# Loads of q, k and v issued from POOL instead of SP, a second staging buffer for k, and q of the first tile in one piece

## The chip, the cores and the metric

The kernel runs on one core of one Trainium2 chip. The metric is device time in microseconds (us) of one execution; before the change it is 709.55 us, the median of three runs (708.3 to 709.76).

## What is computed

Attention with a bias, followed by two layers of the mixture kind (two matrices in, one out), over B = 2 batches, H = 8 heads, S = 576 positions, D = 64:

```python
scores = scale * np.matmul(q, k.transpose(0, 1, 3, 2))            # scale = 1/sqrt(D)
x = (log1p(abs(i - j)) / log1p(max(i, 1)))[..., None]
bias = np.maximum(x @ w1 + b1, 0.0) @ w2                          # 32 hidden, one column per head
attn = softmax(scores + bias.transpose(2, 0, 1)[None])
x = (attn @ v) as [1152 tokens, 512]
x = (x @ w_a) * (x @ w_b) @ w_out                                 # 512 -> 1536 -> 512
return silu(x @ w_gate) * (x @ w_val) @ w_out2
```

## The kernel before

All arithmetic is in 32-bit floats. Matmuls that need it are split into a high part that TensorE takes quickly and a low part (names that end in `a` and `b`, or in `h` and `l`), so a product is three matmuls.

**Bias units.** The bias depends on a row and a column position alone. It is made in 36 units of 16 rows for all 8 heads (`Bias.make`, line 132): four hidden layers `hd` (L122 on VectorE or L124 on ScalarE), matmuls against w2 on TensorE (L146), scaled copies into a tile `bt` (L128, L130), and a write of that tile to a scratch tensor `bias_d` in DRAM (L159, 295.5 KB, on SP's queue). Four units (32 to 35) are made ahead of everything; they are the bias rows of the tile t = 4.

**Attention.** The heads go in four pairs p = 0 to 3. The 1152 query columns (both batches) are cut into five tiles, in the order t = 4, 0, 1, 2, 3: t = 4 has 64 queries of each batch (192 columns of `qd` with 64 columns of zeros), the others 128 of each. A step is one (t, p), tile by tile, p inside; there are 20 steps. A step with t = 4 does both batches at once, in one half; the others have two halves. Before each half `make()` makes up to three bias units (three for each of the first four halves, then two and one in turn) until all 36 are there. The rows of a tile's bias can only be loaded once the units of that tile have been written.

In a step, for each of the two heads j, a tile `bt` (four buffers in all, L264's input) is loaded from `bias_d` on SP's queue: for t = 4 in two loads of 64 rows each (L355, 144 KB each, four loads in a step), else in one load of 128 rows (L352, 288 KB, two loads in a step). Then `scores` makes the matmuls of q and k (L259) in PSUM, VectorE adds the bias and takes the minimum (L264; the "score reduction" below), ScalarE makes the exponentials (L270), TensorE transposes them (L288), copies go to `ee` (L275, L277), TensorE multiplies with v (L299), and `finish` divides by the sums.

**Loads of heads.** `Heads` loads what a pair needs, all on SP's queue. `load_k(p)` (L187, 576 KB) fetches k into one staging buffer `kr` and splits it at once: a cast to `ka` (L172 on VectorE or L174 on ScalarE) and a subtraction to `kb` (L176, VectorE). `load_q(p, t)` (L182) does the same for q of one step (96 KB for t = 4, else 128 KB). `load_v(p)` (L192, 640 KB) fetches v, which isn't split; each pair has its own v tile.

At the start SP issues the constants `cs`, the logarithms `LW`, k0 and q of step 0, then v0. In step idx, after the step's bias row loads, SP issues k of the next pair (first tile only), q of the next step, and v of the next pair (first tile only). The lines of the loop:

```python
with tc.issue_after(load.ins):
    if idx + 1 < len(steps):
        if t == ORDER[0] and p < H // 2 - 1:
            heads.load_k(p + 1)
        heads.load_q(*steps[idx + 1])
        if t == ORDER[0] and p < H // 2 - 1:
            heads.load_v(p + 1)
```

`tc.issue_after(ins)` keeps what the block issues on the engine of `ins` behind `ins`, on that engine alone. The order of instructions on each engine is otherwise set by the framework's planner when the program is built, from its own estimates; each engine then takes its instructions strictly in that order and waits on semaphores. `Share` decides, from a running sum of estimated costs, whether a cast or copy goes to VectorE or ScalarE.

**The two layers** (`moe`, L404 the matmuls, L424 to L429 and L453 to L458 around them) follow; POOL computes there (L458) and at the very start.

Of the kernel before, what the change touches and what calls it, by code (L numbers as in the profile page):

```python
# [9 lines left out]
F32 = mybir.dt.float32  # L10
# [7 lines left out]
P = 128  # L18
B, H, S, D = 2, 8, 576, 64
# [9 lines left out]
ORDER = (4, 0, 1, 2, 3)  # L29
# [43 lines left out]
class Share:  # L73


    def __init__(self):
        self.spent = [0.0, 0.0]
# [14 lines left out]
class Bias:  # L92
# [7 lines left out]
    def __init__(self, tc, stack, cst, lm, bias_d, heads, share):  # L100
        nc = self.nc = tc.nc
        self.tc, self.bias_d, self.share = tc, bias_d, share
        bc = self.bc = stack.enter_context(tc.tile_pool(name="bm", bufs=1, side="right"))
        cs = bc.tile([P, 214], F32, name="cs")
        LW = self.LW = bc.tile([P, S], F32, name="LW")
        nc.sync.dma_start(cs, cst)
        last_load = nc.sync.dma_start(LW, lm)
        one = bc.tile([P, 1], F32, name="one")
        nc.gpsimd.memset(one, 0.0)
        nc.scalar.activation(one, one, AF.Exp)  # L110
        W1, B1, self.W2, PS, self.RE = cs[:, 0:1], cs[:, 1:2], cs[:, 2:34], cs[:, 34:178], cs[:, 178:214]
        with tc.high_priority():
            bp = self.bp = bc.tile([P, 144], F32, name="bp")
            nc.vector.tensor_scalar(bp, PS, B1, None, op0=ALU.mult)
            ready = nc.vector.tensor_scalar(LW, LW, W1, None, op0=ALU.mult)
        with tc.issue_after(ready.ins), tc.issue_after(last_load.ins):
            heads.load_k(0)
            heads.load_q(0, ORDER[0])

    def hidden(self, dst, n, m):  # L120
        if self.share.on_dve(n, DFAST):
            self.last = self.nc.vector.tensor_scalar(dst, self.LW[:, :n], self.bp[:, m : m + 1], 0.0, op0=ALU.add, op1=ALU.max)  # L122
        else:
            self.nc.scalar.activation(dst, self.LW[:, :n], AF.Relu, bias=self.bp[:, m : m + 1])  # L124
# [37 lines left out]
class Heads:  # L162


    def __init__(self, tc, pool, qd, kd, vd, share):
        self.nc, self.pool, self.d, self.got, self.share = tc.nc, pool, (qd, kd, vd), {}, share

    def split(self, raw, tags, bufs):
        w = raw.free_size() if hasattr(raw, "free_size") else raw.shape[1]
        hi, lo = (self.pool.tile([P, w], F32R, tag=x, name=x[:2], bufs=bufs) for x in tags)  # L170
        if self.share.on_dve(w, DFAST):
            self.nc.vector.tensor_copy(hi, raw)  # L172
        else:
            self.nc.scalar.copy(hi, raw)  # L174
        self.share.dve(w)
        self.nc.vector.tensor_tensor(lo, raw, hi.bitcast(F32), op=ALU.subtract)  # L176
        return hi, lo

    def load_q(self, p, t):
        s, n = (0, 192) if t == 4 else (192 + 256 * t, 256)  # L180
        raw = self.pool.tile([P, n], F32, tag=f"rawq{n}", name="rawq", bufs=1 if t == 4 else 2)
        self.nc.sync.dma_start(raw, self.d[0][p][:, s : s + n])  # L182
        self.got["q", p, t] = self.split(raw, (f"qa{n}", f"qb{n}"), 2)

    def load_k(self, p):
        kr = self.pool.tile([P, B * S], F32, tag="kr", name="kr", bufs=1)
        self.nc.sync.dma_start(kr, self.d[1][p])  # L187
        self.got["k", p] = self.split(kr, (f"ka{p}", f"kb{p}"), 1)

    def load_v(self, p):  # L190
        vv = self.pool.tile([P, B, 10, D], F32, tag=f"vv{p}", name="vv", bufs=1)
        self.nc.sync.dma_start(vv, self.d[2][p])  # L192
        self.got["v", p] = vv


# [35 lines left out]
def attention(ctx, tc, a4, heads, share, bias, units, bias_d, xh, xl, weights, ident):  # L231

    nc = tc.nc
    with (
# [6 lines left out]
        def bias_rows(h, t, n):  # L241
            e = bias_d[t][h]
            return bass.AP(tensor=e.tensor, offset=e.offset + 15, ap=[[16 * BW, n // 16], [BW - 1, 16], [1, S]])
# [3 lines left out]
        def scores(p, q, blocks, bt, sums):  # L247

            ka, kb = heads.got["k", p]
            qa, qb = q  # L250
            ps = ps2.tile([P, 2, 2, 512], F32, tag="big", name="ps")
            es = a4.tile([P, 2, S], F32, tag="es", name="es", bufs=3)
            for hf in range(2):
                for m, (lt, rt) in enumerate(((qa, ka), (qa, kb), (qb, ka))):
                    for j in range(2):
                        r = slice(64 * j, 64 * j + 64)
                        for n, (c0, b) in enumerate(blocks):
                            k0 = S * b + 288 * hf
                            nc.tensor.matmul(  # L259
                                ps[:, j, hf, :288], lt[r, c0 : c0 + P], rt[r, k0 : k0 + 288], start=m + n == 0, stop=m + n == len(blocks) + 1  # L260
                            )
            for j in range(2):
                nm = a4.tile([P, 1], F32, tag="nm", name="nm", bufs=4)
                nc.vector.tensor_tensor_reduce(  # L264
                    out=es[:, j].rearrange("p (a j) -> p a j", a=2), in0=ps[:, j, :, :288], in1=bt[j].rearrange("p (a j) -> p a j", a=2),
                    op0=ALU.add, op1=ALU.min, scale=-0.125, scalar=3.0e38, accum_out=nm,
                )
                share.dve(S, 1.3)
                share.act(S, 190.0)
                nc.scalar.activation(es[:, j], es[:, j], AF.Exp, bias=nm, scale=-1.0, accum_out=sums[:, j : j + 1])  # L270
            return es.rearrange("p h k -> p (h k)")
# [20 lines left out]
        def values(p, pu, ee, blocks):  # L292

            vv = heads.got["v", p]
            for cols, b, o in blocks:
                n = cols.stop - cols.start
                for kc in range(5):
                    for j in range(2):
                        nc.tensor.matmul(pu[64 * j : 64 * j + 64, o : o + n], vv[:, b, 5 * j + kc], ee[:, 4 * j + kc, cols], start=kc == 0, stop=kc == 4)  # L299
# [30 lines left out]

        for u in UNITS[:FIRST]:
            units.make(u, bank)
        heads.load_v(0)
        rest = list(UNITS[FIRST:])
        steps = [(p, t) for t in ORDER for p in range(H // 2)]
        half = 0

        def make():
            nonlocal half
            for _ in range(MADE[half] if half < len(MADE) else 0):  # L340
                if rest:
                    units.make(rest.pop(0), bank)
                    if not rest:
                        bias.close()
                        weights.pool = ctx.enter_context(tc.tile_pool(name="wpa2", bufs=1, side="right"))
            half += 1

        for idx, (p, t) in enumerate(steps):
            bt = [a4.tile([P, S], F32, tag="bias", name="bt", bufs=4) for j in range(2)]
            for j in range(2):  # L350
                if t < 4:
                    load = nc.sync.dma_start(bt[j], bias_rows(2 * p + j, t, P))  # L352
                else:
                    for b in range(B):
                        load = nc.sync.dma_start(bt[j][64 * b : 64 * b + 64], bias_rows(2 * p + j, 4, 64))  # L355
            with tc.issue_after(load.ins):
                if idx + 1 < len(steps):
                    if t == ORDER[0] and p < H // 2 - 1:
                        heads.load_k(p + 1)
                    heads.load_q(*steps[idx + 1])  # L360
                    if t == ORDER[0] and p < H // 2 - 1:
                        heads.load_v(p + 1)
                if idx == len(steps) - 2:
                    weights.load(3)
            q = heads.got["q", p, t]
            pu = ps0.tile([P, 512], F32, tag="pu", name="pu")
            if t < 4:
                sums = a2.tile([P, 2 * B], F32, tag="sums", name="sums")
                for b in range(B):
                    make()  # L370
                    es = scores(p, q, [(P * b, b)], bt, sums[:, 2 * b : 2 * b + 2])
                    values(p, pu, transposed(es), [(slice(0, P), b, P * b)])
            else:
                sums = a2.tile([P, 2], F32, tag="sums4", name="sums")
                make()
                es = scores(p, q, [(64 * b, b) for b in range(B)], bt, sums)
                values(p, pu, transposed(es), [(slice(64 * b, 64 * b + 64), b, 64 * b) for b in range(B)])
            finish(p, t, pu, sums)
# [159 lines left out]
```

## Time and profile before

| | |
|---|---|
| median of three runs | 709.55 us (708.3 to 709.76) |
| profiled execution, its own time | 708.51 us |
| its span, first to last instruction | 706.7 us |
| TensorE (PE) busy | 663.4 us, 94% of the span |
| VectorE (DVE), ScalarE (ACT), POOL busy | 65%, 46%, 2% |
| DMA | 71.44 MB, mean 101 GB/s; all of the program's on one queue |
| attention | to about 245 us; then the two layers |

An engine's busy time counts its instructions, not its waits. "Idle before" an instruction is how long its engine did nothing just ahead of it, and the arrow names what ended that. A granted clock of 1.00 is TensorE at 2.4 GHz, 0.50 at 1.2 GHz. The DMA share is the mean over the core's 16 DMA engines, so a quarter can be four engines that never rest.

### The profile page before, as it was taken

Reading aid. Unit: us, or ns where it says so; the run is one execution under the profiler, and the core shown is the slowest. Engines: PE = TensorE matmul, PEld = TensorE weight load, DVE = VectorE, ACT = ScalarE, POOL = GpSimd, SP = SyncE. Lnnn points to the kernel's source line nnn. Section 1 sums busy time; section 2 is a strip of 40 time slices with the busy share of each in tenths; the row PEclk is TensorE's granted clock in tenths of the full one; section 3 lists DMA queues with packets and bytes.
Section 4 is the critical chain, followed back from the end, with each engine's and each line's share of the span. In section 5 each row is a group of like instructions: output and inputs, shape, how many; then the busy total and the mean of one; then the engine's idle time right before and its main releaser. Section 6 shows DMA issues by size and latency. Waiting matters only on the chain.

```text
span 706.7 us, 11756 instructions
## 1 busy us (share of the span) xinstructions
PE 663.4 (94%) x4584; PEld 584.3 (83%) x4584; DVE 460.4 (65%) x1034; ACT 322.4 (46%) x675; POOL 13.9 (2%) x19
## 2 busy tenths in 40 slices
PE   6457799999999989999999999999999999999997
PEld 3133455655776879999999999999999999999997
DVE  5445688886777969999938961289923992342222
ACT  5514667775676747555415432265513641221110
POOL 0000000000000000000000001202000000000000
PEclk9767999999999999999999999999999999999999
DMA  4663554544335315444413430033510540000111
GB/s 134 186 199 123 155 145 132 155 125 115 100 101 156 102 60 179 148 151 128 142 59 94 146 119 1 1 107 124 163 55 1 157 141 0 1 1 1 45 45 45
DMA packets 27096, 71.44 MB, mean 101 GB/s; under 512 B 2720, under 2 KB 6944, under 8 KB 27040
## 3 DMA queue, kind: packets, MB, share of 16 engines
q1 hardware_dynamic: 27040, 70.68, 32.6%
q8 instruction: 36, 0.59, 0.3%
q14 instruction: 20, 0.16, 0.1%
HBM read 57.42 MB, written 13.25 MB: 100 GB/s over the span
## 4 chain that ended last, share of the span: by engine, by line
PE 83%; DMA 8%; DVE 4%; ACT 2%; issue 2%; SPq 1%; DVEq 0%; ACTq 0%
PE p L404 42%; PE po L404 21%; PE pu L299 6%; PE tp L146 5%; PE tp L288 5%; PE ps L259 4%; DMA rawq<-in_qd 3%; DMA kr<-in_kd 3%; DMA raw<-in_wm 1%; DMA bias_d<-bt 1%; PE tp L311 1%; DVE es L264 1%; DVE hd L122 1%; ACT es L270 1%; DMA LW<-in_lm 0%
## 5 line engine op out<-in xcount | busy, mean ns | idle before, releaser
L425 DVE TENSOR_TENSOR g<-p,g 128x384 f32<-128x384 f32 x72 | 40.0, 556 | 140.2 <-PE p L404 140.1
L404 PE MATMUL p<-xh,wh 128*128 128x384 f32 x288 | 96.7, 336 | 2.2 <-ACT g L424 2.2
L404 PE MATMUL p<-xl,wh 128*128 128x384 f32 x288 | 96.5, 335 | 0.0
L404 PE MATMUL po<-gh,wl 128*128 128x384 f32 x288 | 96.5, 335 | 0.0
L404 PE MATMUL p<-xh,wl 128*128 128x384 f32 x288 | 96.4, 335 | 0.0
L404 PE MATMUL p<-yh,wl 128*128 128x384 f32 x288 | 96.4, 335 | 0.0
L404 PE MATMUL p<-yh,wh 128*128 128x384 f32 x288 | 96.3, 335 | 0.0
L404 PE MATMUL po<-gl,wh 128*128 128x384 f32 x288 | 96.3, 335 | 0.0
L404 PE MATMUL p<-yl,wh 128*128 128x384 f32 x288 | 96.3, 334 | 0.0
L404 PE MATMUL po<-gh,wh 128*128 128x384 f32 x288 | 95.9, 335 | 0.0
L424 ACT ACTIVATE g<-p 128x384 f32<-128x384 f32 x72 | 35.3, 491 | 110.7 <-PE p L404 110.6
L427 ACT CAST gh<-g 128x384 fp32r<-128x384 f32 x72 | 37.0, 514 | 83.1 <-DVE g L425 83.1
L288 PE MATMUL tp<-ident,es 128*128 128x128 f32 x324 | 56.0, 294 | 15.3 <-ACT es L270 14.3
L146 PE MATMUL tp<-hd,cs 128*32 128x264 f32 (+17 forms) x352 | 54.2, 525 | 15.0 <-DVE hd L122 8.3
L288 PEld LDWEIGHTS tp<-ident,es 128*128 128x128 f32 x324 | 35.1, 144 | 39.5 <-issue 18.5
L299 PE MATMUL pu<-ee,vv 128*64 128x128 f32 (+1 forms) x800 | 65.2, 274 | 2.1 <-ACT ee L277 1.8
L270 ACT ACTIVATE es<-es,nm 128x576 f32<-128x576 f32 x72 | 55.5, 771 | 23.5 <-DVE nm L264 22.9
L299 PEld LDWEIGHTS pu<-ee,vv 128*64 128x64 f32 x800 | 45.8, 138 | 22.9 <-issue 9.5
L227 ACT CAST wh<-m 128x512 fp32r<-128x512 f32 x72 | 44.3, 621 | 43.3 <-DVE m L226 39.9
L221 ACT ACTIVATE m<-raw 128x512 f32<-128x512 f32 x72 | 48.4, 677 | 33.5 <-DVE wl L228 30.0
L264 DVE CUSTOM_DVE_ANT_0 es<-ps,bt 128x576 f32<-128x576 f32 x72 | 51.9, 752 | 13.0 <-DMA bt<-bias_d 11.7
L404 PEld LDWEIGHTS p<-xh,wh 128*128 128x128 f32 x288 | 54.1, 188 | 2.5 <-ACT g L424 2.5
(60 smaller groups left out, 1153.4 us busy)
## 6 DMA issues: line engine op xcount, KB each, us to landing
raw<-in_wm SPq DMA_DIRECT2D x72, 512.0 KB
bias_d<-bt SPq DMA_DIRECT2D x36, 295.5 KB
bt<-bias_d SPq DMA_DIRECT2D x32, 288.0 KB
vv<-in_vd SPq DMA_DIRECT2D x4, 640.0 KB
kr<-in_kd SPq DMA_DIRECT2D x4, 576.0 KB
bt<-bias_d SPq DMA_DIRECT2D x16, 144.0 KB
out_t<-acc SPq DMA_DIRECT2D x12, 192.0 KB
rawq<-in_qd SPq DMA_DIRECT2D x16, 128.0 KB
```

Of the source, the lines that this page charges most:

```text
L146: nc.tensor.matmul(ps[32 * cg : 32 * cg + 32, :w], self.W2, hd[cg][:, w * a : w * a + w], start=True, stop=True)
L221: nc.scalar.activation(m, hi.bitcast(F32), AF.Abs)
L227: nc.scalar.copy(wh[:, i], m)
L259: nc.tensor.matmul(ps[:, j, hf, :288], lt[r, c0 : c0 + P], rt[r, k0 : k0 + 288], start=m + n == 0, stop=m + n == len(blocks) + 1)
L264: nc.vector.tensor_tensor_reduce(out=es[:, j].rearrange("p (a j) -> p a j", a=2), in0=ps[:, j, :, :288], in1=bt[j].rearrange("p (a j) -> p ...
L270: nc.scalar.activation(es[:, j], es[:, j], AF.Exp, bias=nm, scale=-1.0, accum_out=sums[:, j : j + 1])
L288: nc.tensor.transpose(tp[:, n], es[:, o : o + P], ident)
L299: nc.tensor.matmul(pu[64 * j : 64 * j + 64, o : o + n], vv[:, b, 5 * j + kc], ee[:, 4 * j + kc, cols], start=kc == 0, stop=kc == 4)
L404: nc.tensor.matmul(ps, lt, rt, start=first and n == 0, stop=last and n == len(parts) - 1)
L424: nc.scalar.activation(g, pp[0], AF.Silu if layer else AF.Copy)
L425: nc.vector.tensor_tensor(g, pp[1], g, op=ALU.mult)
L427: nc.scalar.copy(gh, g)
```

## The change

The change moves the loads of q, k and v from SP's queue to POOL's; SP keeps the constants, the bias writes, the row loads, the weights and the output. k is fetched (`fetch_k`) apart from its split (`split_k`), into two staging buffers. q of the first tile comes for all four pairs in one load (384 KB, rows of 192 columns) with one cast and one subtraction over 768 columns. At the start k0, q and k1 are fetched, then v0 and v1; step p of the first tile splits k(p+1), and fetches k(p+2) and v(p+2). The order after `ready` (the scaling of `LW` on VectorE), which held for the first split, is dropped; the one that is left, after `last_load`, names an instruction of SP and so doesn't bind POOL.

```diff
-        with tc.issue_after(ready.ins), tc.issue_after(last_load.ins):
-            heads.load_k(0)
+        with tc.issue_after(last_load.ins):
+            heads.fetch_k(0)
             heads.load_q(0, ORDER[0])
+            heads.fetch_k(1)
+            heads.split_k(0)
...
+        self.queue, self.raw_k = tc.nc.gpsimd, {}
...
     def load_q(self, p, t):
-        s, n = (0, 192) if t == 4 else (192 + 256 * t, 256)
-        raw = self.pool.tile([P, n], F32, tag=f"rawq{n}", name="rawq", bufs=1 if t == 4 else 2)
-        self.nc.sync.dma_start(raw, self.d[0][p][:, s : s + n])
-        self.got["q", p, t] = self.split(raw, (f"qa{n}", f"qb{n}"), 2)
-
-    def load_k(self, p):
-        kr = self.pool.tile([P, B * S], F32, tag="kr", name="kr", bufs=1)
-        self.nc.sync.dma_start(kr, self.d[1][p])
-        self.got["k", p] = self.split(kr, (f"ka{p}", f"kb{p}"), 1)
+
+        if t == 4:
+            raw = self.pool.tile([P, H // 2, 192], F32, tag="raw4", name="raw4", bufs=1)
+            self.queue.dma_start(raw, self.d[0][:, :, :192].rearrange("p d n -> d p n"))
+            q = self.split(raw.rearrange("d p n -> d (p n)"), ("qa4", "qb4"), 1)
+            for i in range(H // 2):
+                self.got["q", i, t] = [x[:, 192 * i : 192 * i + 192] for x in q]
+        else:
+            raw = self.pool.tile([P, 256], F32, tag="rawq", name="rawq", bufs=2)
+            self.queue.dma_start(raw, self.d[0][p][:, 192 + 256 * t : 448 + 256 * t])
+            self.got["q", p, t] = self.split(raw, ("qa", "qb"), 2)
+
+    def fetch_k(self, p):
+        self.raw_k[p] = self.pool.tile([P, B * S], F32, tag="kr", name="kr", bufs=2)
+        self.queue.dma_start(self.raw_k[p], self.d[1][p])
+
+    def split_k(self, p):
+        self.got["k", p] = self.split(self.raw_k[p], (f"ka{p}", f"kb{p}"), 1)
 
     def load_v(self, p):
         vv = self.pool.tile([P, B, 10, D], F32, tag=f"vv{p}", name="vv", bufs=1)
-        self.nc.sync.dma_start(vv, self.d[2][p])
+        self.queue.dma_start(vv, self.d[2][p])
...
-        heads.load_v(0)
+        for p in range(2):
+            heads.load_v(p)
...
+            if p + 1 < H // 2 and t == ORDER[0]:
+                heads.split_k(p + 1)
+                if p + 2 < H // 2:
+                    heads.fetch_k(p + 2)
+                    heads.load_v(p + 2)
+            if idx + 1 < len(steps) and steps[idx + 1][1] != ORDER[0]:
+                heads.load_q(*steps[idx + 1])
             with tc.issue_after(load.ins):
-                if idx + 1 < len(steps):
-                    if t == ORDER[0] and p < H // 2 - 1:
-                        heads.load_k(p + 1)
-                    heads.load_q(*steps[idx + 1])
-                    if t == ORDER[0] and p < H // 2 - 1:
-                        heads.load_v(p + 1)
                 if idx == len(steps) - 2:
                     weights.load(3)
```

## Rows read from the trace of the kernel before

**Rows 1.** Windows: start:end, length; busy us (instructions) PE, PEld, DVE, ACT, POOL; PEclk, DMA share, GB/s.

```profile
22.00:90.00 68.00, 40.16 (x353) 22.96 (x353) 35.87 (x98) 29.15 (x68) 0.00 (x0) 0.79 0.57 167
90.00:165.00 75.00, 73.81 (x680) 42.93 (x677) 62.05 (x175) 52.73 (x126) 0.00 (x0) 0.98 0.49 140
...
245.00:707.00 462.00, 455.58 (x2646) 453.38 (x2644) 286.35 (x560) 174.12 (x325) 13.20 (x12) 1.00 0.25 81
...
32.00:76.00 44.00, 28.70 (x236) 16.49 (x236) 23.52 (x58) 16.54 (x39) 0.00 (x0) 0.74 0.52 160
```

**Rows 2.** Chain that ended last: start us, us, what; two of its load pieces.

```profile
35.99 11.15 DMA kr<-in_kd
48.28 9.59 DMA rawq<-in_qd
```

**Rows 3.** Timeline, 40 to 62 us: start us, us, instruction [idle before, what ended it].

```profile
47.16 0.76 DVE L172 CAST ka<-kr 128x1152 fp32r<-128x1152 f32 x1 [7.58 <-DMA kr<-in_kd]
47.41 0.35 ACT L174 CAST qa<-rawq 128x192 fp32r<-128x192 f32 x1 [10.78 <-DMA rawq<-in_qd]
...
51.23 4.13 PE L146 MATMUL tp<-hd,cs 128*32 128x512 f32 x12 [8.34 <-DVE hd L122]
...
57.95 0.35 ACT L174 CAST qa<-rawq 128x192 fp32r<-128x192 f32 x1 [5.61 <-DMA rawq<-in_qd]
...
61.44 0.66 PE L288 MATMUL tp<-ident,es 128*128 128x128 f32 x4 [4.30 <-ACT es L270]
```

**Rows 4.** Windows of 2 us, columns as in rows 1.

```profile
4.00:6.00 2.00, 0.41 (x1) 0.18 (x2) 1.43 (x3) 1.20 (x2) 0.00 (x0) 1.00 1.04 348
...
44.00:46.00 2.00, 0.00 (x0) 0.00 (x0) 0.00 (x0) 0.00 (x0) 0.00 (x0) 0.76 0.26 106
...
60.00:62.00 2.00, 0.56 (x4) 0.42 (x4) 0.80 (x3) 2.00 (x6) 0.00 (x0) 1.00 0.26 101
```

**Rows 5.** Page, DMA issues: out<-in, engine, count, KB each.

```profile
bias_d<-bt SPq DMA_DIRECT2D x36, 295.5 KB
...
vv<-in_vd SPq DMA_DIRECT2D x4, 640.0 KB
kr<-in_kd SPq DMA_DIRECT2D x4, 576.0 KB
bt<-bias_d SPq DMA_DIRECT2D x16, 144.0 KB
```

**Rows 6.** Timeline, score reductions: second of step p = 0, first of p = 1, 2, 3, next tile.

```profile
32.60 0.76 DVE L264 CUSTOM_DVE_ANT_0 es<-ps,bt 128x576 f32<-128x576 f32 x1 [2.45 <-DMA bt<-bias_d]
...
52.65 0.75 DVE L264 CUSTOM_DVE_ANT_0 es<-ps,bt 128x576 f32<-128x576 f32 x1
...
64.27 0.75 DVE L264 CUSTOM_DVE_ANT_0 es<-ps,bt 128x576 f32<-128x576 f32 x1
...
75.35 0.75 DVE L264 CUSTOM_DVE_ANT_0 es<-ps,bt 128x576 f32<-128x576 f32 x1
...
81.45 0.76 DVE L264 CUSTOM_DVE_ANT_0 es<-ps,bt 128x576 f32<-128x576 f32 x1 [2.61 <-DMA bt<-bias_d]
```

**Rows 7.** Waits of SP's queue: who for whom, us in total, times, longest.

```profile
SPq L355 <- DMA bt<-bias_d: 6.7, 6, 1.9
```

**Rows 8.** Timeline of the start: first cast of k, first scores, first bias writes.

```profile
6.29 0.76 DVE L172 CAST ka<-kr 128x1152 fp32r<-128x1152 f32 x1 [0.58 <-DMA kr<-in_kd]
...
9.02 0.85 PE L259 MATMUL ps<-ka,qa 64*128 64x288 f32 x4
...
10.59 8.46 SPq L159 DMA_DIRECT2D bias_d<-bt  x4
```

**Rows 9.** Groups of instructions, 0 to 90 us: shapes, count, busy us, mean ns, idle before.

```profile
L176 DVE TENSOR_TENSOR kb<-kr,ka 128x1152 fp32r<-128x1152 f32 x4 | 5.4, 1355 | 0.0
...
L176 DVE TENSOR_TENSOR qb<-rawq,qa 128x192 fp32r<-128x192 f32 x4 | 1.4, 354 | 3.2 <-ACT qa L174 3.2
L174 ACT CAST qa<-rawq 128x192 fp32r<-128x192 f32 x4 | 1.4, 343 | 16.4 <-DMA rawq<-in_qd 16.4
```

## The prediction

> **What bounds the kernel now.** I read the stages first, as windows of the whole span [rows 1]. From 245 us on, and from 90 to 165 us, TensorE is busy for 98% of the time and more at full granted clock: there the kernel is bound by matmuls, which the change doesn't touch. In the stretch from 22 to 90 us TensorE is busy for 40.2 of 68.0 us, at a mean granted clock of 0.79. The 27.8 us of idle time there are all that a change of loads can win, apart from what comes back of the clock, which I count in no term. (The first 22 us make the first four bias units.) This stretch holds the four steps of the first tile (t = 4; p = 0 to 3) and the start of the next tile.
>
> Second, the chain of waits says what the stretch hangs on: loads of k and q, 10 to 11 us each from issue to use [rows 2]. Third, the timeline shows what a late load does. VectorE takes its instructions in order and stands 7.58 us before the cast of k for p = 2; ScalarE stands 10.78 us before the cast of q; behind them lie the hidden layers of the next bias unit, so TensorE stands 8.34 us for them. The same again a step later: ScalarE 5.61 us for q, TensorE 4.30 us for the exponentials queued behind it [rows 3]. These two TensorE bubbles, 12.6 us, are the wait that the change aims at.
>
> Fourth, why these loads are late. In windows of 2 us the DMA share sits at 0.26 with 101 to 106 GB/s around 44 and 60 us, whereas at 4 us it is full, at 348 GB/s [rows 4]. A quarter of 16 engines is four engines at about 25 GB/s each. What moves then are the bias row loads of t = 4: their outermost dimension has 64/16 = 4 members, and I read from the share that each of these loads runs on four engines, the same four each time. So per step these four engines carry, from the sizes [rows 5] (1 KB = 1.024 kB): four row loads of 144 KB over four engines, 147 kB on each, 5.9 us at 25 GB/s; k, 576 KB over 16, 1.5 us; v, 640 KB, 1.6 us; q (192 columns, 96 KB), 0.25 us; three bias writes of 295.5 KB, 0.76 us each, 2.3 us. Sum 11.5 us. The measured distance from one step's first score reduction to the next is 64.27 - 52.65 = 11.6 and 75.35 - 64.27 = 11.1 us [rows 6]. That agreement is what I build on: the first tile is paced by four DMA engines that everything passes, with k and q behind the rows on one queue. SP also waited six times, 6.7 us in total, for a landing before it could issue another row load [rows 7], and k, q and v stood behind that.
>
> **The change part by part.**
>
> *k, q and v on POOL's queue.* In this stretch POOL computes nothing, so nothing of its own stands ahead of them. They no longer pass the bias writes and row loads on SP, nor SP's waits. On POOL they stand in program order: k0, q of all four pairs, k1, then v0 and v1, then k2 with v2, k3 with v3. v waits for nothing. k2 needs the staging buffer of k0, free when the subtraction behind the cast at 6.29 us is done [rows 8]; k3 needs k1's, and behind it on POOL stand only v3 and the q of later tiles, wanted from about 64 us on. So k1, v1, k2 and v2 can move before 22 us, where the bias writes begin at 10.59 us [rows 8]. The bytes on the four engines stay the same; they leave the steps that the four engines pace. If all k, q and v go early, a step costs 5.9 + 2.3 = 8.2 us; if none do, 11.5 us. I take 9.8: of the three steps after the first, k3, v2 and v3 still fall into them, (1.5 + 1.6 + 1.6)/3 = 1.6 us a step on top of 8.2.
>
> *Price at the start.* About 250 kB more (k1 to k3, v1 to v3, three q) pass each engine early, 10 us at 25 GB/s; some of it shares engines with the bias writes and the first rows. Bounds: nothing (the engines are partly idle until 22 us), and 10 us if all goes ahead of the first rows. I take 2 us, nearer to nothing, since most fits before 22 us.
>
> *Second staging buffer.* It lets k(p+1) lie ready when the cast for it comes up. This removes the 7.58 us stand of VectorE. Next late after it are the rows, which is the 9.8 us above.
>
> *One load and one split of q.* Four casts of 0.343 us and four subtractions of 0.354 us [rows 9], 2.8 us, become one pair over 768 columns. The nearest rows are the cast and the subtraction over 1152 columns, 0.76 us [rows 8] and 1.36 us [rows 9]: under 2.1 us, so at least 0.7 us of work goes. But the pair now stands at the start, about 1 us longer there than one quarter was; it is in the 2 us. The 5.61 us stand of ScalarE goes.
>
> *A DMA issue on POOL.* No row of before shows one. Lower bound 0, as on SP, where the issues lie off the path; upper bound, a POOL issue that waits for a running VectorE instruction, 1.36 us at most [rows 9]. For nine loads that is 12 us spread over POOL's queue, which has that slack from k2 on. For VectorE instructions that wait for POOL I take 1 us in all.
>
> The Trainium skill, "SBUF — State Buffer", section "SBUF: two separate sides", speaks against this change: descriptors of a DMA issued on POOL are written by POOL's cores, which are locked out while VectorE runs certain copies, and it advises SP or ScalarE instead. It gives 0.62 us alone and 3.1 us beside such a copy; nine loads at that price, as an estimate by that page, would be 22 us more on POOL's queue, and k3 would still come in time for p = 3. No run here shows it yet.
>
> *Sum.* The second reduction of step 0 stands at 32.60 us [rows 6]. With 2 us of start and three steps of 9.8 us the first one of step 3 comes at 32.6 + 2 + 29.4 = 64.0 instead of 75.35 us: 11.35 us earlier. Less 1 us on VectorE: 10.3 us. What follows (6.1 us to the next tile's first reduction at 81.45, then the matmul-bound part) keeps its length. Profiled run: 708.51 - 10.3 = 698.2 us. The median lies 1.04 us above that run: 699.2 us.
>
> Low end: step time 8.2, start free: 57.2 instead of 75.35, 18 us. But from 32 to 76 us TensorE has 28.7 us of work in 44 us [rows 1], so no more than some 15 us can go at its clock there, and a little beyond if that rises from 0.74: 692 us.
>
> **The rivals.**
> 1. The loads don't leave the steps. k, q and v still come while rows move, and the step stays at 11.5 us; only the bubble of step 1 goes. 32.6 + 2 + 34.5 = 69.1, gain 6.2, less 1: 5.2 us, 704.3 us. For it: the four engines move every byte either way. Against it: v waits for nothing, and k has two buffers.
> 2. The queue was not it. Order on the compute engines sets the pace, another wait takes the place: 709.5 us. For it: exponentials also wait for the reductions, which wait for rows. Against it: the loads end the longest waits of [rows 3]. The Trainium skill, "DMA: Bandwidth & Descriptors", section "Issuing engines are not separate DMA queues", says much the same: another issuing engine saves issue time alone. By that rule the time would hardly move; the trace has the loads behind SP's waits, which is more than issue time.
> 3. Slower: POOL is slow to give out loads. If each takes d us on POOL, k0 and the first scores come about d later, unit matmuls stand behind these scores in TensorE's order (scores from 9.02 us, before the first bias write [rows 8]), and each later step waits for k and v in turn, 2d: 32.6 + d + 3 x 2d. At d = 6 that is 74.6, no gain; at d = 7 it is 81.6, 6.3 us late, 715.8 us. It decides from about 6.1 us per load. Against it: 1.36 us is the longest that VectorE's rows give reason for. For it: no row shows POOL's price, and the q load comes in 512 pieces.
>
> **How the numbers follow.** Forecast 0.60 (692 to 703), rival 1 0.15, rival 2 0.08, rival 3 0.17. Faster by over 0.2% (1.4 us, about what can be told from no change): 0.60 + 0.15 = 0.75; within: 0.08; slower: 0.17. The range goes from 692 to 711 us: it leaves out some 0.06 below and most of rival 3, some 0.13, above.
>
> **What would show it.** Right: SP issues only bias writes and row loads; no cast of k or q preceded by more than 2 us of idle time after 22 us; the first reductions of steps 1 to 3 some 9.8 us apart, the last near 64 us; TensorE's idle time from 22 to 90 us down by about 10 us; the part after 245 us unchanged in length. Wrong: distances near 11.5 us (rival 1); the same start of the mixture layers with other waits (rival 2); first bias write later than 14 us, or POOL rows of several us per load (rival 3). I'd be wrong too if row loads slow down beyond what bytes say once two queues share their four engines.

## The result

The changed kernel takes 691.09 us (median of four runs, 690.63 to 692.3) against 708.92 us for the kernel before on the same chip: ratio 0.9752, 95% interval 0.9731 to 0.9772. That is 17.8 us less. The forecast was 10.3 us less, and its lower end, 692 us, lies just above the measured median. The profiled execution has a span of 689.5 us, 17.2 us under that of before, and these 17.2 us are laid out below. In the run all_on_sp further down one of four executions took 816.3 us at a granted clock of 0.75, and it is left out there.

The profile after, first the windows of the stage that the forecast was about (columns as in [rows 1]; the third line is the stretch from step p = 1 to p = 3 of the first tile).

```profile
0.00:22.00 22.00, 14.32 (x112) 6.10 (x112) 15.58 (x31) 13.21 (x22) 8.88 (x20) 1.00 0.91 327
22.00:90.00 68.00, 56.16 (x508) 30.57 (x506) 43.94 (x127) 38.52 (x86) 1.08 (x2) 0.95 0.45 138
...
39.78:62.10 22.32, 21.75 (x194) 10.11 (x195) 14.08 (x40) 12.67 (x27) 0.00 (x0) 1.00 0.39 123
```

From 22 to 90 us TensorE's idle time fell from 27.8 to 11.8 us, and the mean granted clock rose from 0.79 to 0.95 [rows 1]. The DMA share of the first 22 us was 0.46 in the kernel before and is 0.91 here. From 39.78 to 62.1 us TensorE is busy for 97% of the time at full clock.

The score reductions, which answer to [rows 6] (timeline: second of step 0, first of steps 1, 2, 3 and of the next tile):

```profile
34.03 0.76 DVE L276 CUSTOM_DVE_ANT_0 es<-ps,bt 128x576 f32<-128x576 f32 x1 [1.83 <-DMA bt<-bias_d]
...
39.78 0.76 DVE L276 CUSTOM_DVE_ANT_0 es<-ps,bt 128x576 f32<-128x576 f32 x1
...
52.18 0.76 DVE L276 CUSTOM_DVE_ANT_0 es<-ps,bt 128x576 f32<-128x576 f32 x1
...
62.14 0.76 DVE L276 CUSTOM_DVE_ANT_0 es<-ps,bt 128x576 f32<-128x576 f32 x1 [0.15 <-PE ps L271]
...
68.03 0.76 DVE L276 CUSTOM_DVE_ANT_0 es<-ps,bt 128x576 f32<-128x576 f32 x1 [1.52 <-DMA bt<-bias_d]
```

The loads as POOL issues them (timeline of POOL):

```profile
1.31 0.68 POOL L197 DMA_DIRECT2D kr<-in_kd  x1 [0.33 <-issue]
1.99 0.77 POOL L186 DMA_DIRECT2D raw<-in_qd  x1
...
3.18 0.57 POOL L197 DMA_DIRECT2D kr<-in_kd  x1
3.74 2.13 POOL L204 DMA_DIRECT2D vv<-in_vd  x4
...
11.03 0.54 POOL L197 DMA_DIRECT2D kr<-in_kd  x1 [4.09 <-DVE kb L179]
...
15.19 0.68 POOL L197 DMA_DIRECT2D kr<-in_kd  x1 [3.63 <-DVE kb L179]
```

All of k, q of the first tile and v is issued by 15.9 us, ahead of the first row load (24.4 us), even v of p = 2 and 3, which the program names only in steps 0 and 1. The stands of [rows 3] are gone: after 22 us no cast of k or q waits for its load.

Where the 17.2 us come from, by the reductions in both traces and the first matmul of the layers (244.60 and 229.40 us):

| stretch | before | after | gained | forecast |
|---|---|---|---|---|
| start to second reduction of step 0 | 32.60 | 34.03 | -1.43 | -2 |
| to first reduction of step 3 | 42.75 | 28.11 | 14.64 | 13.35 |
| to first reduction of the next tile | 6.10 | 5.89 | 0.21 | 0 |
| to first matmul of the layers | 163.15 | 161.37 | 1.78 | 0 |
| layers | 462.10 | 460.10 | 2.00 | 0 |
| VectorE held up by POOL | | | | -1 |
| sum | | | 17.20 | 10.35 |

The 14.64 us are nearly all in the first of their three distances. From step 0's second reduction to step 1's first one it is 20.05 us before and 5.75 us after. The other two distances are 11.62 and 11.08 us before, 12.40 and 9.96 us after.

### The profile page after: what moved, and what is told of

It reads as the page before. It is cut to its first block, busy times and chain, and to the rows that moved or that the text cites. A ratio compares the mean times of both kernels' runs of the same rounds, so it can differ in the third digit from the quotient of the medians.

```text
span 689.5 us, 11753 instructions
## 1 busy us (share of the span) xinstructions
PE 661.9 (96%) x4584; PEld 581.4 (84%) x4584; DVE 461.6 (67%) x1034; ACT 321.5 (47%) x669; POOL 28.7 (4%) x44
## 4 chain that ended last, share of the span: by engine, by line
PE 89%; DMA 6%; DVE 2%; ACT 1%; issue 1%; POOL 1%; SPq 1%; DVEq 0%; POOLq 0%; ACTq 0%
PE p L418 44%; PE po L418 22%; PE pu L311 7%; PE tp L300 6%; PE ps L271 5%; PE tp L148 5%; DMA bt<-bias_d 2%; DMA rawq<-in_qd 1%; DMA raw<-in_wm 1%; DMA bias_d<-bt 1%; DVE es L276 1%; PE tp L323 1%; DVE hd L124 1%; ACT ee L289 0%; SPq L368 0%
## 5 line engine op out<-in xcount | busy, mean ns | idle before, releaser
L148 PE MATMUL tp<-hd,cs 128*32 128x264 f32 (+17 forms) x352 | 56.6, 488 | 10.0 <-ACT hd L126 5.5
L233 ACT ACTIVATE m<-raw 128x512 f32<-128x512 f32 x72 | 48.5, 678 | 32.9 <-DVE wl L240 30.2
L300 PEld LDWEIGHTS tp<-ident,es 128*128 128x128 f32 x324 | 34.7, 142 | 30.2 <-issue 17.2
```

Of the source, the lines that this page charges most:

```text
L148: nc.tensor.matmul(ps[32 * cg : 32 * cg + 32, :w], self.W2, hd[cg][:, w * a : w * a + w], start=True, stop=True)
L233: nc.scalar.activation(m, hi.bitcast(F32), AF.Abs)
L300: nc.tensor.transpose(tp[:, n], es[:, o : o + P], ident)
```

## The experiments

The theory after the result: k, q and v arrive before their casts come up, because they were fetched ahead of the rows; then the matmuls pace the first tile. Open was which part does it: POOL's queue, the new order, the second buffer or the single q load. And the four DMA engines of [rows 4] were read from a share, not tried.

In the table "free" means that q, k and v are not kept behind the rows of their step, and "new" the order of the change.

| kernel | queue | order of loads | k buffers | q of first tile | us |
|---|---|---|---|---|---|
| before | SP | behind the rows | 1 | four loads | 708.9 |
| not_behind_rows | SP | free | 1 | four loads | 704.6 |
| pool_alone | POOL | free | 1 | four loads | 698.3 |
| sp_one_k | SP | new | 1 | one load | 699.3 |
| one_k_buffer | POOL | new | 1 | one load | 696.3 |
| q_four | POOL | new | 2 | four loads | 695.6 |
| all_on_sp, all_on_sp_2 | SP | new | 2 | one load | 691.0, 691.5 |
| after | POOL | new | 2 | one load | 691.1 |

**POOL's queue undone** (all_on_sp; all_on_sp_2 is the same kernel again).

```diff
-        self.queue, self.raw_k = tc.nc.gpsimd, {}
+        self.queue, self.raw_k = tc.nc.sync, {}
```

> The changed kernel (691.1 us) with q, k and v back on SP's queue; the new order, two k buffers and the single q load of the first tile stay. Theory A (a queue of its own is needed: on SP the later k and v stand behind bias writes and row loads again): k of p = 1 and v early, k of p = 2 and 3 late again, some 697 to 704 us. Theory B (order and buffers alone do it): 690 to 693 us. Theory C (the queue is all of it): 707 to 711 us.

> The changed kernel with q, k and v on SP's queue once more, for an undisturbed profile and a narrower interval. Theory B (order and buffers do all of it): 690 to 693 us; all loads of k and v issued before the first row load, step 1's first reduction near 40 us. Theory A (a queue of its own is worth something on top): 694 us or more.

Measured: 691.04 us (the middle one of three; ratio to before 0.9749, interval 0.9718 to 0.9779) and 691.5 us (0.9761, 0.9741 to 0.9781). Theory B: the order, the buffers and the single load of q do all of it, and POOL's queue on top of them adds nothing that can be measured. SP's timeline in all_on_sp_2 shows why:

```profile
1.65 0.42 SPq L197 DMA_DIRECT2D kr<-in_kd  x1
...
2.59 0.51 SPq L197 DMA_DIRECT2D kr<-in_kd  x1
3.14 2.15 SPq L204 DMA_DIRECT2D vv<-in_vd  x4
...
10.61 0.33 SPq L197 DMA_DIRECT2D kr<-in_kd  x1
12.54 0.63 SPq L161 DMA_DIRECT2D bias_d<-bt  x1
14.77 0.34 SPq L197 DMA_DIRECT2D kr<-in_kd  x1
...
24.75 2.37 SPq L368 DMA_DIRECT2D bt<-bias_d  x4
```

The last k is issued at 14.77 us, 10 us ahead of the first row load, so there is nothing on SP for a load to stand behind.

**POOL's queue alone** on the kernel before (pool_alone).

```diff
-        self.nc.sync.dma_start(kr, self.d[1][p])
+        self.nc.gpsimd.dma_start(kr, self.d[1][p])
```

and likewise for q and v. Since `issue_after(load.ins)` binds the engine of that load alone, POOL's loads are free of it.

> The kernel before (708.9 us) with its loads of q, k and v on POOL's queue and nothing else changed: one k buffer, q of the first tile in four loads, k fetched at its split. Theory A: the loads start as soon as buffers are free, so most of the gain, 692 to 698 us, with k of p = 2 at most a few us late. Theory B (order and buffers do it): 706 to 711 us. Theory C: 690 to 693 us.

Measured: 698.32 us, ratio 0.9843 (0.9819 to 0.9867), just above theory A's range. So the move to POOL, which also frees the loads of the order behind the rows, is by itself worth some 11 us of the 18. k of p = 1, 2 and 3 goes out at 8.88, 19.56 and 27.68 us, each behind the split that frees the one buffer; step 0's reductions are later (32.7 and 37.6 us), and step 3's first one comes at 62.9 us, nearly as after. But the next tile's first one comes at 73.9 in place of 68.0 us. At the first matmul of the layers pool_alone is still 3.5 us behind the changed kernel, and its layers are 3.9 us longer (464.0 against 460.1 us; see below).

**The order alone** on the kernel before (not_behind_rows).

```diff
-            with tc.issue_after(load.ins):
-                if idx + 1 < len(steps):
+            if idx + 1 < len(steps):
...
+            with tc.issue_after(load.ins):
```

> The kernel before with one thing undone: its loads of k, q and v are no longer kept behind the row loads of their step on SP's queue (one k buffer, four q loads, SP's queue). If that order was the cause: they go ahead of the rows as soon as buffers are free, 692 to 700 us, like the kernel with POOL's queue alone (698.3 us). If buffers or the queue are the cause: 705 to 710 us.

Measured: 704.64 us, ratio 0.9939 (0.9918 to 0.9961): in neither range, and just under that of buffers or queue. So this order is not the cause by itself. Three k and all v go early, but k of p = 3 has no buffer until the rows are on their way, and then stands on SP among them (chain of waits, then VectorE's timeline):

```profile
39.51 12.23 DMA kr<-in_kd
```

```profile
51.77 0.76 DVE L172 CAST ka<-kr 128x1152 fp32r<-128x1152 f32 x1 [11.02 <-DMA kr<-in_kd]
```

One late load brings back an 11 us stand, as long as any of [rows 3]. It stands in VectorE's order ahead of step 1's reduction, which comes at 53.91 us, later than before (52.65).

**One k buffer**, on POOL (one_k_buffer) and on SP (sp_one_k, with the SP line above as well).

```diff
-        self.raw_k[p] = self.pool.tile([P, B * S], F32, tag="kr", name="kr", bufs=2)
+        self.raw_k[p] = self.pool.tile([P, B * S], F32, tag="kr", name="kr", bufs=1)
```

> The changed kernel with one staging buffer for k in place of two. If the second buffer is needed for k to come ahead of the rows: k of p = 1 waits for the split of k0 (11 us), p = 2 and 3 come each after a split, after 20 us, into the row loads; 695 to 700 us. If one buffer is enough because each split follows its load at once: 690 to 693 us.

> The changed kernel with q, k and v on SP's queue and one k buffer. If two buffers make the queue not matter, one buffer makes it matter: k of p = 2 and 3 then stand on SP among row loads, and it lies well above POOL's 696.3 us, at 700 to 706 us. If the queue never matters: 695 to 698 us.

Measured: 696.33 us on POOL (0.9828, 0.9808 to 0.9847), 699.33 us on SP (0.9877, 0.9862 to 0.9892). The second buffer is worth some 5 us on POOL and 8 on SP; 1.8 us of either lie in the layers, which are 461.9 and 461.7 us long with one buffer against 460.1 and 459.9 with two. On SP it went better than the 700 to 706 us expected, but the mechanism is there: the last k is issued at 36.24 us, behind row loads, and VectorE stands for it.

```profile
36.24 0.58 SPq L197 DMA_DIRECT2D kr<-in_kd  x1
36.86 14.11 SPq L368 DMA_DIRECT2D bt<-bias_d  x8
```

```profile
44.96 0.76 DVE L175 CAST ka<-kr 128x1152 fp32r<-128x1152 f32 x1 [8.23 <-DMA kr<-in_kd]
```

So the parts replace one another. With one buffer a queue of its own is worth 3.0 us (699.3 to 696.3) or 6.3 us (704.6 to 698.3), and in either pair the layers are equal within 0.5 us. With two buffers and the loads first it is worth 0.4 us at most, within the intervals.

**q of the first tile in four loads** (q_four).

```diff
+            raw = self.pool.tile([P, 192], F32, tag="rawq192", name="rawq", bufs=1)
+            self.queue.dma_start(raw, self.d[0][p][:, :192])
+            self.got["q", p, t] = self.split(raw, ("qa192", "qb192"), 2)
...
-            if idx + 1 < len(steps) and steps[idx + 1][1] != ORDER[0]:
+            if idx + 1 < len(steps):
```

> The changed kernel with q of the first tile in four loads and four splits again, one pair at a time, as before the change; queue, order of k and v and the two buffers stay. If the single load matters only through 0.7 us of work: 690 to 693 us. If it is what takes q of p = 1 to 3 off the row loads' way: late casts of q again, 695 to 702 us. If its 384 KB delayed the start: step 0's reductions about 1.5 us earlier, 689 to 690 us.

Measured: 695.61 us, ratio 0.9813 (0.9792 to 0.9834). By its number that is the second range, but the sign of it is missing: no cast of q is late. In the profiled execution, which at 693.97 us is the fastest of the four, the attention part is no longer than in the changed kernel (first matmul of the layers at 227.7 against 229.4 us), and step 0's second reduction stands at 33.81 us. The layers are longer, 464.3 against 460.1 us. What the single load itself does is thus within some 2 us there; the rest lies in the layers, whose order of instructions a new build changed (see below). The three longer executions have no profile.

**Row loads on 16 engines** (rows16_before on the kernel before, rows16_after on the changed one). The queries within a tile are put in another order, so that the load's outermost dimension has 16 members; the order of rows in the packing of q and in the output goes with it.

```diff
-ap=[[16 * BW, n // 16], [BW - 1, 16], [1, S]]
+ap=[[BW - 1, 16], [16 * BW, n // 16], [1, S]]
...
-[S * b + P * t + r for b in range(B) for r in range(n // 2)]
+[S * b + P * t + 16 * a + c for b in range(B) for c in range(16) for a in range(n // 32)]
```

> The kernel before with the order of queries inside a tile permuted, so that a bias row load has 16 members in its outermost dimension in place of 4 (first tile) or 8. If the four engines that carried these loads paced the first tile, its DMA time of a step falls from 11.5 to 7.1 us (5.9 us of rows become 1.5) and the loads of k and q behind them come earlier: the first reductions of steps 1 to 3 lie 8 to 9.5 us apart, 696 to 703 us in all. If the share of 0.25 came from something else, 707 to 711 us with the distances at 11 us.

> The changed kernel with the same 16-member row loads. Theory A (after 40 us TensorE paces, ahead of it the rows of steps 0 and 1 on four engines): the second reduction of step 0 comes near 29.5 in place of 34.0 us, the rest follows at the same distances, 685 to 688 us. Rival (rows pace all steps of the first tile in the changed kernel too): distances between steps 1, 2 and 3 fall below 9 us from 12.4 and 9.9, under 684 us. Rival (rows matter nowhere any more): 690 to 692 us.

Measured: 691.0 us (0.9733, 0.9698 to 0.9767) and 683.34 us (0.9626, 0.9594 to 0.9658). The same bytes over 16 engines win as much as the whole change does, more than the 6 to 13 us expected. From 24 to 25 us only row loads of step 0 are on their way in both kernels (windows of the kernel before, then of rows16_before):

```profile
24.00:25.00 1.00, 0.00 (x0) 0.00 (x0) 0.00 (x0) 0.73 (x2) 0.00 (x0) 1.00 0.24 94
```

```profile
24.00:25.00 1.00, 0.01 (x1) 0.00 (x0) 0.00 (x0) 1.00 (x4) 0.00 (x0) 1.00 0.85 247
```

So these loads did run on a quarter of the engines, and spread they run on most of them.

In rows16_before the first reductions of steps 1 to 3 stand at 44.75, 52.01 and 62.70 us, distances of 7.3 and 10.7 us against 11.6 and 11.1. Of the 16.3 us between the two profiled executions 12.7 lie ahead of step 3's first reduction and 5.2 between it and the layers, where the rows of the other tiles are spread too; the layers are 1.6 us longer.

The four engines thus paced step 0 and the way from step 1 to step 2. They did not pace the way from step 2 to step 3, which hardly changes: in the kernel before, TensorE is busy for nearly all of it, at a DMA share of 0.31 (window of the kernel before):

```profile
64.27:75.35 11.08, 10.94 (x98) 5.66 (x98) 7.21 (x24) 6.89 (x16) 0.00 (x0) 0.79 0.31 90
```

And the longest distance, from step 0 to step 1, falls only from 20.1 to 17.0 us, since q and k still come behind the rows (timeline of ScalarE in rows16_before):

```profile
39.52 0.35 ACT L174 CAST qa<-rawq 128x192 fp32r<-128x192 f32 x1 [7.61 <-DMA rawq<-in_qd]
```

In rows16_after the second reduction of step 0 comes at 30.2 us, 3.8 us earlier, and the distances between steps 1, 2 and 3 are 11.8 and 10.0 us, against 12.4 and 10.0; from step 0's second reduction to step 1's first it is 5.45 us, against 5.75. The distances are those of theory A, but the time is under its range and in that of the first rival, because another 2.7 us are won between step 3's first reduction and the layers. In the changed kernel, then, the rows pace step 0's reductions. Step 1's second one and the next tile's first one still wait 1.5 us each for rows, but the distances between steps 1, 2 and 3 depend little on them.

**Two bias units a step in place of three** (two_units, on the changed kernel).

```diff
-MADE = (3, 3, 3, 3, *(2, 1) * 6, 2)
+MADE = (2, 2, 2, 2, *(2, 1) * 8)
```

> The changed kernel (691.1 us) with two bias units in place of three made in each of the first four halves, the others later (2 and 1 in turn). If TensorE paces steps 1 to 3 of the first tile: a unit is 2 us of matmuls (12.0 us for six in the changed kernel's trace), so the distances of first reductions fall from 12.4 and 9.9 to about 10.2 and 7.9 us, while the total stays within 1.5 us, since the matmuls only move. If the row loads pace them: distances unchanged.

Measured: 695.26 us, ratio 0.9821 (0.9802 to 0.9841). Timeline, first reductions of steps 1, 2, 3 and of the next tile:

```profile
40.16 0.76 DVE L276 CUSTOM_DVE_ANT_0 es<-ps,bt 128x576 f32<-128x576 f32 x1 [0.72 <-PE ps L271]
...
48.84 0.76 DVE L276 CUSTOM_DVE_ANT_0 es<-ps,bt 128x576 f32<-128x576 f32 x1 [0.57 <-PE ps L271]
...
56.65 0.74 DVE L276 CUSTOM_DVE_ANT_0 es<-ps,bt 128x576 f32<-128x576 f32 x1
...
71.83 0.76 DVE L276 CUSTOM_DVE_ANT_0 es<-ps,bt 128x576 f32<-128x576 f32 x1 [2.84 <-DMA bt<-bias_d]
```

The distances fall to 8.7 and 7.8 us with two units, so the units' work paces these steps in the changed kernel, with TensorE at 97% in the window above. The total did not stay within 1.5 us: the next tile needs the eight units of its rows, and its first reduction now lies 15.2 us behind step 3's in place of 5.9.

**v of p = 2 and 3 late again** (v_late, on the changed kernel).

```diff
-                    heads.load_v(p + 2)
+                    heads.queue = nc.sync
+                    with tc.issue_after(load.ins):
+                        heads.load_v(p + 2)
+                    heads.queue = nc.gpsimd
```

> The changed kernel with v of p = 2 and 3 fetched on SP's queue behind the row loads of their step again. If early bytes are what puts step 0 back (second reduction 34.0 against 32.6 us before): near 32.8 us, and the total unchanged or up to 1.5 us less. If it is VectorE's longer work at the start: still near 34 us; v's 3.2 us on each of the four engines then falls into the steps and costs 0 to 3 us.

Measured: 694.04 us, ratio 0.9803 (0.9785 to 0.982). Fewer bytes move before 22 us (254 against 327 GB/s), and yet step 0's reductions come at 34.0 and 38.2 us, later by 4 us and not earlier. So the start is not put back by early bytes. That VectorE is busier there (15.58 against 12.87 us of the first 22) is the other explanation; it was not tried alone, and v_late, with 14.59 us, speaks for the order of the instructions rather than their sum. The traces show where the delay enters. The row loads of step 0 wait for the last of four bias writes, which goes out at 18.53 us before, at 21.07 us in the changed kernel and at 25.30 us in v_late. In the chain of waits of v_late the split of k of p = 3 stands ahead of it on VectorE:

```profile
21.79 0.77 DVE ka L175
...
22.59 1.36 DVE kb L179
23.95 0.44 DVE hd L124
...
25.30 3.00 DMA bias_d<-bt
```

In the changed kernel the same chain leads through the split of a q of the next tile (15.82 us). No run moves these splits alone, so this is read from the chains and not tried.

**Both together without POOL** (sp_rows16: the SP line and the 16-member rows on the changed kernel).

> The changed kernel with q, k and v on SP's queue and the 16-member row loads: the order and the buffers without POOL, and rows on all engines. If the queue doesn't matter here either: 682 to 685 us, as with POOL's queue (683.3 us); if it does: 686 us or more.

Measured: 683.13 us, ratio 0.965 (0.9632 to 0.9669), the same as on POOL's queue (683.34). This is the fastest version seen, 8 us under the changed kernel, with or without POOL.

## Why the prediction was right and wrong

**What bounded the kernel: right for the stands, wrong for the pace of every step.** Late k and q behind rows on four engines held the first tile up to step 2's first reduction. rows16_before shows the four engines directly, and every kernel that brings k early wins. But the agreement that the forecast builds on, a sum of 11.5 us against distances of 11.6 and 11.1 us, was chance in the second distance: TensorE was busy for 10.94 of its 11.08 us, and with rows on 16 engines it still is 10.7 us.

**Step time 9.8 us: right in its sum by luck, wrong in its mechanism.** Three steps took 28.1 us in place of 29.4, and the start cost 1.4 us in place of 2. But the step that was to fall from 11.5 to 9.8 us because bytes leave the four engines did not do so: the last two distances together fell by 0.3 us. The gain is that of the stand for k and q, 14.3 us in the first distance. That one took 5.75 us (39.78 - 34.03), close to the 5.9 us of four row loads by accident, since with rows on 16 engines it is still 5.45 us. It is the time of step 1's score matmuls, which have to wait until VectorE frees their tile in PSUM and then run at 0.50 of the clock; the last four of them stand behind transposes of step 0 (timeline of TensorE in the changed kernel, then its windows):

```profile
34.85 0.85 PE L271 MATMUL ps<-ka,qa 64*128 64x288 f32 x4 [1.76 <-DVE nm L276]
```

```profile
34.00:36.00 2.00, 1.15 (x10) 1.15 (x12) 1.64 (x6) 0.87 (x2) 0.00 (x0) 0.50 0.26 101
36.00:38.00 2.00, 2.00 (x17) 1.61 (x15) 0.10 (x1) 0.30 (x1) 0.00 (x0) 0.50 0.66 213
```

The other two took 12.4 and 10.0 us, also by TensorE, with three units a step. I had weighed TensorE's 28.7 us of work in 44 us only as a bound for the whole stretch and not asked what a single step costs there. The same bound put the lower end at 692 us. In the changed kernel it held, with 13.2 us won up to step 3's first reduction against some 15; in rows16_after 17.9 us are won there, so it was too tight, since part of the work in it ran at 0.50 of the clock.

**"What follows keeps its length": wrong, and the largest miss.** 4.0 us of the missing 6.9 us lie behind step 3's first reduction (0.21, 1.78 and 2.00 us), a term that I had put at nothing. It is what brings the median under the lower end of 692 us: without it the time would be some 695 us. (The rest is 1.3 us in the steps, 0.6 us at the start and the 1 us for VectorE.) Of the 2.00 us in the layers the trace names the place. Before, TensorE waits once there, for the first activation of ScalarE, whose turn comes behind weight casts that wait for VectorE:

```profile
258.09 1.22 ACT L227 CAST wh<-m 128x512 fp32r<-128x512 f32 x2 [3.18 <-DVE m L226]
...
260.20 0.86 ACT L424 ACTIVATE g<-p 128x384 f32<-128x384 f32 x2
```

```profile
260.73 0.45 PE L404 MATMUL p<-xh,wh 128*128 128x384 f32 x1 [2.16 <-ACT g L424]
```

In the changed kernel that activation stands ahead of the casts, and no such wait is there:

```profile
238.96 0.48 ACT L438 ACTIVATE g<-p 128x384 f32<-128x384 f32 x1
...
241.66 0.62 ACT L239 CAST wh<-m 128x512 fp32r<-128x512 f32 x1 [0.80 <-DVE m L238]
```

The wait is in the profiles of before, pool_alone, rows16_before, not_behind_rows, one_k_buffer, sp_one_k and q_four (1.6 to 2.9 us; layers 461.7 to 464.3 us) and in none of after, all_on_sp_2, rows16_after, sp_rows16, two_units and v_late (459.9 to 461.5 us). The change has no line there: the planner orders ScalarE anew in each build. The layers differ by up to 4.4 us between the kernels; at most 2.9 us of that is this wait, and the rest I have not traced. That the planner alone does it is inferred, since no pair of kernels differs in that order only. Comparisons of these kernels finer than some 4 us speak of it too, unless the layers are set apart. The 1.99 us (0.21 + 1.78) between step 3's first reduction and the layers I can only place; their cause stays open. 1.35 us of it lies in the stretch from that reduction to the first one of the next tile's third step, 29.45 us long before (from 75.35 us, mean granted clock 0.94) and 28.10 us after (from 62.1 us, 1.00).

**VectorE held up by POOL, 1 us: not seen.** A POOL issue takes 0.53 to 1.00 us, and the kernel is as fast with the loads on SP. Rival 3 needed 6 us per load. The page "SBUF — State Buffer" of the Trainium skill, section "SBUF: two separate sides", gives 3.1 us for a POOL DMA beside a VectorE copy. No issue here took that: one of 0.54 us falls into the 6 us from 8 to 14 us, in which VectorE was busy throughout, and the longest, 1.00 us at 18.84 us, stands beside a cast of k. The page's figure is for the whole DMA and ours for its issue alone.

**Moving to POOL's queue: the wrong credit.** I put the gain down to loads that no longer pass SP's waits. That holds for pool_alone, but in the changed kernel the order and the second buffer had already taken every load ahead of the waits. Rival 2 said that the queue was not it; right of the queue, wrong of the time, for the same edit carried the order and the buffer. The rule of "DMA: Bandwidth & Descriptors" in the Trainium skill, section "Issuing engines are not separate DMA queues", that another issuing engine saves issue time alone, agrees with 691.5 against 691.1 us, and falls short where a load stands behind row loads on an in-order queue, where the queue was worth 3.0 and 6.3 us. Rival 1 (steps stay at 11.5 us, and only one stand goes) came nearer than the forecast for the last two distances, 11.2 us in the mean, though TensorE and not the four DMA engines set them; it failed in the first.

## What to carry to other kernels

When a trace shows a transfer that is late, ask first where it stands in its queue's order and whether its buffer was free, and only then which queue it is on: loads that go out before the queue begins to wait need no queue of their own. A DMA share that sits at a plain fraction, here a quarter, points at an access pattern whose outermost dimension uses that many of the engines, and spreading it was worth as much as the whole reordering. A sum that agrees with a measured distance is no proof of what paces it; look in that stretch for the engine that is full. When a bound goes, work out per step what the next engine needs, and allow for a planner that reorders places the change doesn't touch.

## What the runs showed of the hardware that was not expected

While k, v and q came in (with a bias write going out from 12 us on), the DMA engines moved 416 to 417 GB/s over 6 us, more than the 348 GB/s of [rows 4], whether the loads stood on POOL's queue or on SP's (windows of the changed kernel, then of all_on_sp_2):

```profile
8.00:14.00 6.00, 5.22 (x50) 2.67 (x47) 6.00 (x12) 2.46 (x5) 0.54 (x1) 1.00 1.02 417
```

```profile
8.00:14.00 6.00, 6.00 (x55) 3.12 (x47) 6.00 (x12) 2.43 (x5) 0.00 (x0) 1.00 1.01 416
```
